# Long convolution by FFT and a gated MLP in one kernel: the first half of a batch's transform moved beside the second half of the one before it, and the last inverse step in two matmul passes instead of three for 17 of 48 tiles

## The chip, the core and the metric

One core of a Trainium2 chip runs the whole program. Its engines are named as in the profile: PE (TensorE, matmuls), PEld (its weight loads), DVE (VectorE), ACT (ScalarE), POOL (GpSimd) and SP (SyncE, which here only issues DMAs). The metric is device time in microseconds (us) of one execution, the median of the runs shown.

## The reference

```python
X = np.fft.rfft(x, axis=1)                       # x: 8 batches, 3008 positions, 256 channels
Y = X * (filt_r + 1j * filt_i)[None]
h = np.fft.irfft(Y, n=3008, axis=1).reshape(24064, 256) @ w_in     # 256 x 2048
out = (h * (1.0 / (1.0 + np.exp(-1.702 * h)))) @ w_out             # 2048 x 256
```

All is float32. A sequence of 3008 is transformed as 64 x 47, with dense matrices.

## The kernel before

The work of a batch `b` is a transform (`fft`, four steps of matmuls with pointwise work between), then six tiles `t` of up to 512 tokens, for which `signal` or `turned_signal` makes the last inverse step, and `mlp` the two products of the MLP. A tile has 16 chunks `fc`; a chunk has 6 matmuls into `h` (L784) and 6 into `o` (L808), two ACT gelus (L787, L788) and one DVE subtraction (L789). Every matmul runs in float32r; to keep float32's precision, operands are split into a high and a low part, and a product is the sum of high x high, high x low and low x high. `mm3` does that in three matmuls. A packed form does it in two: where the contraction fills only 64 partitions, high and low parts of the data are stacked in 128 partitions, and one matmul makes two halves of 64 rows that ACT and DVE then add.

**The transform.** `packed` (batches 2 to 7, counted from 0) is its first half: `fetch` loads a piece of `x` (512 KB, six per batch), `butterfly` makes sums and differences of it on POOL (L519), `split` divides them into high and low parts (ACT L525, POOL L526), `transform` multiplies (L537) and sends the result to DRAM (`a_d`). The second half has 16 steps `i`: `forward(i)` multiplies (`s2`, L588), ACT and DVE merge the two halves (`merge`, L596, L597), DVE multiplies with the filter, POOL adds (L612), DVE and POOL split the product again into `zy` (L616, L617); `backward(i)` multiplies `zy` (`i2`, L588), merges and stores to DRAM (`b_d`). The data of a batch goes through `a_d` and `b_d`, so its steps follow each other; the first half of batch `b + 1` began when the second half of batch `b` had ended.

**The last inverse step.** `turned_signal` loads `br` from `b_d`, splits it (ACT L739, POOL L740), multiplies it with `mm3` (L305 to L307, `i1`), transposes on DVE (L748, `zt`), turns the tile through DRAM (`z_d`, one store and four loads into `y`), and splits it (`split_off`: ACT L719, POOL L720).

**What sets the order.** The program is written as generators: at each chunk a table says how many steps of the transform (`COSTS`) and of the coming tiles (`due`, offsets `at` in chunks) are recorded. A scheduler then places each instruction in its engine's queue; each engine runs its queue strictly in that order, and waits at its head. Tiles in SBUF come from rings: `raw` (seven buffers of 4 KB a partition, among them the pieces of `x`) and `half` (seven of 2 KB). PE, too, runs in the recorded order.

Of the kernel before, what the change touches and what calls it, by code (L numbers as in the profile page):

```python
# [24 lines left out]
COSTS = [[0.746] * 12 + [1.212] * 2 + LATER] + [[0.8] * 4 + [0.675] * 24 + [1.3] * 2 + LATER] * 7  # L25
# [5 lines left out]
def _tables():  # L31
# [72 lines left out]
    tabs = [t1_0, d_0, e_0, np.eye(P), sign, t1, t1_s, t2, de]  # L104
# [4 lines left out]
WIDTHS = {"t1_0": P, "d_0": 2 * Q, "e_0": 192, "eye": P, "sign": NS, "t1": P, "t1_s": P, "t2": P, "de": 4 * Q}  # L109
# [58 lines left out]
def tile_kernel(  # L168
# [291 lines left out]
    def fft(b):  # L460
# [106 lines left out]
        yield from packed() if b > 1 else thrice()  # L567
# [68 lines left out]
        keep(4)  # L636
        if b == 1:
            nc.gpsimd.memset(zy[0].bitcast(F32), 0.0)
        for i in range(2):
            load(i)  # L640
            load_f(i)

        for i in range(2):
            yield
        for i in range(17):
            if i < 16:
                yield from forward(i)
            if i:
                yield from backward(i - 1)
        b_of[b] = b_d  # L650
# [63 lines left out]
    def split_off(y, m, q, to=None):  # L714

        to = y[:, :, m, q] if to is None else to
        src = y[:, 1, m, q].bitcast(F32)
        with tc.issue_after(gelu[-1]):
            nc.scalar.copy(to[:, 0], src)  # L719
        nc.gpsimd.tensor_tensor(to[:, 1], src, to[:, 0].bitcast(F32), ALU.subtract)  # L720

    def turned_signal(b, t, y):
# [20 lines left out]
        zt = sb.tile([P, 8, 4, 32], F32, tag="raw", name=f"zt_{b}_{t}", bufs=7)  # L743
        for m in range(2):
            ps = ring("f", [P, 2, D], f"i1_{b}_{t}_{m}")
            mm3(ps, t2h, t2l, *es[m])
            to = zt[:, :, 2 * m : 2 * m + 2].rearrange("p c q i -> p q c i")
            nc.vector.transpose(to, ps.rearrange("p q (c i) -> p q c i", c=8))  # L748
            yield
        z_d = dram.tile([P, 8, P], F32, tag="z_d", name=f"z_d_{b}_{t}")  # L750
        load_in(z_d, zt.rearrange("p c q i -> p c (q i)"))
        yield
        src = z_d.rearrange("(a j) (k g) e -> g j k a e", a=4, g=4)
        for g in range(4):
            dst = y[32 * g : 32 * g + 32, 1].bitcast(F32)
            load_in(dst.rearrange("p k (a e) -> p k a e", a=4), src[g])
        yield
        for m in range(2):
            if t < 5 or b % 2:
                split_off(y, m, slice(0, 512))  # L760
# [4 lines left out]
            elif t == 5:  # L765
                split_off(y, m, slice(0, 352))
                split_off(y, m, slice(384, 416), y[:, :, m, 352:384])
                split_off(y, m, slice(416, 480), carry[:, :, m])
            yield

    def mlp(b, t, y, nb, sums):
# [7 lines left out]
        def first(fc):  # L779
# [3 lines left out]
            for n, (kc, wk, yk) in enumerate([(k, *q) for k in range(2) for q in ((0, 0), (0, 1), (1, 0))]):  # L783
                nc.tensor.matmul(ps[:, :w], wi_sb[half][:, wk, kc, c], y[:, yk, kc, :w], start=n == 0, stop=n == 5)  # L784
# [53 lines left out]
    ys, t2_two, gelu = {}, [], []  # L838
# [117 lines left out]
```

## Time and profile before

| what | before |
|---|---|
| time, median of 3 runs (lowest to highest) | 2334.91 us (2334.2 to 2335.23) |
| time of the profiled execution | 2334.13 us |
| span of its instructions | 2332.3 us |
| PE busy | 2324.5 us (100%) |
| DVE, ACT, POOL busy | 1607.8, 1439.8, 1128.0 us |
| DMA, mean over the span | 125 GB/s |

The span runs from the first to the last profiled instruction; the time of the execution holds 1.8 us more. "Busy" is the time in which an engine had at least one instruction at work. A matmul's own duration in the profile is longer than the distance to the next one, since matmuls are pipelined, so for PE the distance between starts is what counts.

### The profile page before, as it was taken

The page shows a single profiled execution, that of the slowest core. Times are in us where ns is not written, and L with a number is a line of the kernel's source. Part 1 is how long each engine was busy: PE and PEld are TensorE (multiplying, and loading weights), DVE is VectorE, ACT ScalarE, POOL GpSimd, SP SyncE. Part 2 cuts the span into 40 slices and gives each one's busy share as a digit, 9 for nine tenths or more (in the row PEclk, how much of TensorE's full clock was granted, in tenths as well). Part 3 has the DMA queues.
Part 4 walks back from the last instruction along what each step waited for, and adds up shares of the span by engine and source line. Part 5 has one row for each costly group of instructions (what it writes and reads, how often), then busy time and mean ns, then how long its engine had stood idle before and what let it go on. Part 6 is the DMA issues. An engine that isn't in the chain of part 4 may idle for free.

```text
span 2332.3 us, 32211 instructions
## 1 busy us (share of the span) xinstructions
PE 2324.5 (100%) x10630; PEld 1944.9 (83%) x10630; DVE 1607.8 (69%) x2404; ACT 1439.8 (62%) x2654; POOL 1128.0 (48%) x999
## 2 busy tenths in 40 slices
PE   9999999999999999999999999999999999999999
PEld 7878898888888889888888888988888888888887
DVE  7978866688667885678855887568876688623222
ACT  6666657666675666756676666766657666544443
POOL 3035546466564665556654565736657466311010
PEclk9999999999999999999999999999999999999999
DMA  9265545566455664556545554555655465411100
GB/s 338 82 192 111 111 107 146 134 135 135 109 145 125 144 140 127 154 121 139 127 133 141 133 128 117 153 134 125 138 134 145 118 138 118 101 52 52 57 28 19
DMA packets 189238, 290.75 MB, mean 125 GB/s; under 512 B 18576, under 2 KB 125200, under 8 KB 189072
## 3 DMA queue, kind: packets, MB, share of 16 engines
q1 hardware_dynamic: 112368, 178.20, 26.5%
q0 software_dynamic: 46592, 44.05, 11.4%
q10 hardware_dynamic: 30112, 66.44, 11.1%
q8 instruction: 85, 1.39, 0.3%
q14 instruction: 81, 0.66, 0.1%
HBM read 173.80 MB, written 114.82 MB: 124 GB/s over the span
## 4 chain that ended last, share of the span: by engine, by line
PE 93%; DVE 0%; ACT 0%; issue 0%
PE o L808 42%; PE h L784 42%; PE s L588 2%; PE i L588 2%; PE s L537 1%; PE i L305 1%; PE i L307 1%; PE i L306 1%; PE i L700 0%; PE bt L671 0%; PE s L585 0%; PE s L586 0%; PE i L586 0%; PE i L585 0%; DVE out L816 0%; ACT gh L787 0%
## 5 line engine op out<-in xcount | busy, mean ns | idle before, releaser
L784 PE MATMUL h<-y,wi 128*128 128x512 f32 (+1 forms) x4608 | 1177.3, 385 | 0.1
L784 PEld LDWEIGHTS h<-y,wi 128*128 128x128 f32 x4608 | 858.9, 188 | 165.2 <-DVE gl L789 1.0
L789 DVE TENSOR_TENSOR gl<-h,gh 128x512 fp32r<-128x512 f32 (+1 forms) x768 | 520.7, 678 | 495.4 <-ACT h L788 467.9
L808 PE MATMUL o<-gh,wo 128*128 128x512 f32 (+1 forms) x3072 | 839.2, 385 | 1.2 <-ACT gh L787 1.2
L787 ACT ACTIVATE gh<-h 128x512 fp32r<-128x512 f32 (+1 forms) x768 | 452.2, 589 | 606.6 <-PE h L784 462.9
L808 PEld LDWEIGHTS o<-gh,wo 128*128 128x128 f32 x3072 | 573.4, 188 | 111.6 <-ACT gh L787 1.9
L808 PE MATMUL o<-gl,wo 128*128 128x512 f32 (+1 forms) x1536 | 481.6, 385 | 0.5 <-DVE gl L789 0.5
L788 ACT ACTIVATE h<-h 128x512 f32<-128x512 f32 (+1 forms) x768 | 449.0, 585 | 0.0
L617 POOL TENSOR_TENSOR zy<-c_buf,zy 48x512 fp32r<-48x512 f32 x224 | 316.0, 1411 | 75.0 <-DVE zy L616 63.3
L808 PEld LDWEIGHTS o<-gl,wo 128*128 128x128 f32 x1536 | 287.5, 188 | 56.5 <-DVE gl L789 1.1
L612 POOL TENSOR_TENSOR c_buf<-c_buf,u_buf 112x512 f32<-112x512 f32 x112 | 144.6, 1291 | 229.2 <-DVE c_buf L611 229.2
L574 POOL DMA_DIRECT2D zy<-a_d x224 | 130.3, 586 | 232.5 <-PE s L588 92.9
L740 POOL TENSOR_TENSOR bl<-br,bh 128x512 fp32r<-128x512 f32 x80 | 107.1, 1353 | 246.5 <-ACT bh L739 204.7
L720 POOL TENSOR_TENSOR y<-y 128x512 fp32r<-128x512 f32 (+1 forms) x86 | 105.3, 1230 | 205.2 <-ACT y L719 193.8
L597 DVE TENSOR_TENSOR c_buf<-s,c_buf 48x512 f32<-48x512 f32 x224 | 154.1, 688 | 33.3 <-ACT c_buf L596 28.6
L596 ACT COPY c_buf<-s 48x512 f32<-48x512 f32 x224 | 130.2, 581 | 70.9 <-PE s L588 58.5
L596 ACT COPY b<-i 48x512 f32<-48x512 f32 x224 | 130.1, 581 | 58.4 <-PE i L588 46.5
L597 DVE TENSOR_TENSOR b<-i,b 48x512 f32<-48x512 f32 x224 | 153.8, 687 | 15.1 <-ACT b L596 10.3
L540 DVE TENSOR_TENSOR a<-s,a 64x512 f32<-64x512 f32 x144 | 99.0, 688 | 63.3 <-ACT a L539 60.5
L616 DVE CAST zy<-c_buf 48x512 fp32r<-48x512 f32 x224 | 109.4, 488 | 39.8 <-POOL c_buf L612 34.6
L605 DVE TENSOR_TENSOR u_buf<-c_buf,f_buf 48x512 f32<-48x512 f32 x112 | 110.3, 985 | 3.8
L539 ACT CAST a<-s 64x512 fp32r<-64x512 f32 x144 | 83.7, 581 | 40.8 <-PE s L537 26.6
(126 smaller groups left out, 1789.5 us busy)
## 6 DMA issues: line engine op xcount, KB each, us to landing
f_buf<-fs SPq DMA_DIRECT2D x224, 192.0 KB, 3.4
zy<-a_d POOLq DMA_DIRECT2D x224, 192.0 KB, 3.7
a_d<-a ACTq DMA_DIRECT2D x144, 256.0 KB, 3.0
x<-in_x_dram SPq DMA_DIRECT2D x47, 512.0 KB, 5.5
out_dram<-out SPq DMA_DIRECT2D x43, 512.0 KB, 3.7
b_d<-b ACTq DMA_DIRECT2D x112, 192.0 KB, 2.8
br<-b_d SPq DMA_DIRECT2D x84, 256.0 KB, 4.5
z_d<-zt SPq DMA_DIRECT2D x40, 512.0 KB, 2.7
```

What stands on the lines that cost most here:

```text
L574: nc.gpsimd.dma_start(zy[0][64 * k : 64 * k + 48, i % 2].rearrange("p k s d -> p (k s) d"), src)
L596: nc.scalar.copy(dst[h], ps[o])
L597: nc.vector.tensor_tensor(dst[h], ps[h], dst[h], ALU.add)
L605: nc.vector.tensor_tensor(u2[64:Q], u1[0:48], f_i[0:48], ALU.mult)
L612: nc.gpsimd.tensor_tensor(u1, u1, u2, ALU.add)
L616: nc.vector.tensor_copy(y[h, k], u1[h])
L617: nc.gpsimd.tensor_tensor(y[o, k], u1[h], y[h, k].bitcast(F32), ALU.subtract)
L784: nc.tensor.matmul(ps[:, :w], wi_sb[half][:, wk, kc, c], y[:, yk, kc, :w], start=n == 0, stop=n == 5)
L787: nc.scalar.activation(gh[:, :w], ps[:, :w], AF.Gelu_apprx_sigmoid)
L788: gelu.append(nc.scalar.activation(ps[:, :w], ps[:, :w], AF.Gelu_apprx_sigmoid).ins)
L789: nc.vector.tensor_tensor(gl[:, :w], ps[:, :w], gh[:, :w].bitcast(F32), ALU.subtract)
L808: ins = nc.tensor.matmul(pos[m][:, :w], wb[:, P * m : P * m + P], g[:, :w], start=first_one, stop=last_one)
```

## The change

Three things are edited together.

First, `fft` now gives two generators, the first half and the second (`two`). A list of moments (`steps`, from `SPACED` and `FIRST_LEG`) replaces `COSTS`. From batch 3 on the first half of batch `b` begins while the second half of batch `b - 1` still runs: 4 of its 24 matmul steps lie beside it for batch 3 and 6 for batches 4 to 7, within the last 16 and 24 chunks of it.

Second, the first half gets its own memory, `s1_pool`: two slots for pieces of `x`, three for results, one for the even sums. Before, all these took buffers of the rings `raw` and `half`. `fetch` now runs at odd `n`, when the last split of a slot is recorded.

Third, for the tiles that `is_packed` names (t = 3, 4, 5 of b = 3 to 6, and t = 1 to 5 of b = 7: 17 tiles) `packed_passes` replaces `turned_passes`: four matmuls of 512 columns instead of six, with four merges, and sums and differences on POOL (into `yf`) after the turn through DRAM.

```diff
-COSTS = [[0.746] * 12 + [1.212] * 2 + LATER] + [[0.8] * 4 + [0.675] * 24 + [1.3] * 2 + LATER] * 7
+SPACED = [(0, 0, 32), (16, 4, 20), (24, 6, 17)]
+FIRST_LEG = [0.746] * 12 + [1.212] * 2 + LATER
...
+                s1_pool.append(const.tile([P, 6, 4, D], F32, tag="b_t", name="s1_pool"))
...
-                    xs[c] = raw(f"x_{b}_{c}").rearrange("p (j i) d -> p j i d", j=2)
+                    xs[c] = s1_pool[0][:, c % 2].rearrange("p (j i) d -> p j i d", j=2)
...
-                        if n % 2 == 0:
+                        if n % 2:
                             fetch(n // 2 + 2)
...
+    def is_packed(b, t):
+        return b > 2 and t > 2 or b == B - 1 and t > 0
...
+    def packed_passes(b, t, zt):
...
+        br = [raw(f"br{j}_{b}_{t}") for j in range(2)]
+        for j in range(2):
+            n = NH * j + 4 * t
+            for k in range(2):
+                load_in(br[j][halves(k)], b_of[b][n : n + 4].rearrange("n k d -> k n d"))
+        yield
+        es = {}
+        for m in range(2):
+            for j in range(2):
+                e, src = half(f"z{j}_{b}_{t}_{m}"), br[j][:, 2 * m : 2 * m + 2]
+                with tc.issue_after(gelu[-1]):
+                    nc.scalar.copy(e, src)
+                nc.gpsimd.tensor_tensor(e[64:P], src[64:P], e[64:P].bitcast(F32), ALU.subtract)
+                es[m, j] = e
+            yield
+        zt.append(sb.tile([P, 8, 4, 32], F32, tag="raw", name=f"zt_{b}_{t}", bufs=7))
+        for m in range(2):
+            uv = sb.tile([P, 2, D], F32, tag="half", name=f"uv_{b}_{t}_{m}", bufs=7)
+            for j in range(2):
+                ps, h, o = ring("f", [P, 2, D], f"i1_{b}_{t}_{m}_{j}"), halves(j), halves(1 - j)
+                with tc.issue_after(begin[-1]):
+                    nc.tensor.matmul(ps, t2_w[0][:, j].rearrange("p a c -> p (a c)"), es.pop((m, j)), start=True, stop=True)
+                nc.scalar.copy(uv[h], ps[o])
+                nc.vector.tensor_tensor(uv[h], ps[h], uv[h], ALU.add)
...
+            for j in range(2):
+                ins = nc.gpsimd.tensor_tensor(yj[:, :, j], uv[:, :, 0], uv[:, :, 1], ALU.subtract if j else ALU.add)
...
+            if is_packed(b, t):
+                at = (-8, -4, -3, -2, -1, 0, 1, 2, 4, 8, 9, 10)
```

What moves stands below at one place, the end of tile t = 4 of batch 3, where the second half of the transform of batch 4 ends and the first half of that of batch 5 now runs beside it. In the names, `s2_4_15_1` is batch 4, step 15, half 1; `zy` holds batch 4 here, with `c_buf1`, `c_buf2` and `c_buf0` for steps 13, 14 and 15; `e1_5_5` is the split for batch 5, n = 5, half 1; `y_3_5` is the tile that the MLP takes next. In the changed kernel's lines L523 is `butterfly`, L530 `split`, L632 the sum in `forward`, L637 the split into `zy`, L815 the new sums and differences, L730 `split_off`, L825 the copies of left-over tokens into `y`.

POOL's queue before, from the split of step 13 to that of step 15:

```order
L617 TENSOR_TENSOR zy_1451<-c_buf1_83,zy_1451 48x512 x2
L612 TENSOR_TENSOR c_buf2_84<-c_buf2_84,u_buf0_85 112x512
L617 TENSOR_TENSOR zy_1451<-c_buf2_84,zy_1451 48x512 x2
L720 TENSOR_TENSOR y_3_5_10601<-y_3_5_10601 128x512
L764 CAST y_3_5_10601<-carry_88 128x2x32 x2
L720 TENSOR_TENSOR y_3_5_10601<-y_3_5_10601 128x512
L764 CAST y_3_5_10601<-carry_88 128x2x32 x2
L612 TENSOR_TENSOR c_buf0_82<-c_buf0_82,u_buf1_86 112x512
L519 TENSOR_TENSOR ev_5_0_11240<-x_5_0_11177 128x512
L617 TENSOR_TENSOR zy_1451<-c_buf0_82,zy_1451 48x512 x2
```

and now, from the split of step 14 to that of step 15 and the copies:

```order
L632 TENSOR_TENSOR c_buf2_84<-c_buf2_84,u_buf0_85 112x512
L637 TENSOR_TENSOR zy_1452<-c_buf2_84,zy_1452 48x512 x2
L530 TENSOR_TENSOR e1_5_5_11297<-s1_pool_3223,e1_5_5_11297 64x512
L523 TENSOR_TENSOR s1_pool_3223<-s1_pool_3223 128x512
L815 TENSOR_TENSOR yf_3_5_11075<-uvt_3_5_10962 128x2x256 x2
L632 TENSOR_TENSOR c_buf0_82<-c_buf0_82,u_buf1_86 112x512
L523 TENSOR_TENSOR s1_pool_3223<-s1_pool_3223 128x512
L530 TENSOR_TENSOR e0_5_6_11326<-s1_pool_3223,e0_5_6_11326 64x512
L730 TENSOR_TENSOR y_3_5_10582<-yf_3_5_11075,y_3_5_10582 128x512 x2
L637 TENSOR_TENSOR zy_1452<-c_buf0_82,zy_1452 48x512 x2
L825 CAST y_3_5_10582<-carry_88 128x2x32 x4
```

Between the two splits into `zy` there stood eight POOL instructions, four of them short copies; now there are nine, all long: the split `e1_5_5`, two sums of `x`, another split, the tile's own sums and splits.

SP's queue now, around the load of `x` that the first L523 above reads:

```order
L211 DMA z_d_3_5_10909<-zt_3_5_10785 128x1024
L211 DMA uvt_3_5_10962<-z_d_3_5_10909 32x8x128 x4
L211 DMA f_buf_81<-fs_80 48x1024 x2
L211 DMA s1_pool_3223<-in_x_dram 128x1024
L211 DMA f_buf_81<-fs_80 48x1024 x2
L888 DMA out_0_dram<-out_3_4_11258 256x1x512
```

This load writes the slot that `e1_5_5` reads, and so waits for it. Before, this load went to a free buffer of the ring `raw`.

PE's queue before, up to the second inverse matmul of step 15:

```order
L784 MATMUL h_3_5_1_11153<-y_3_5_10601,wi_0_583 128x512 x6
L588 MATMUL i2_4_15_0_11089<-zy_1451,de_sb_79 128x512
L808 MATMUL o_3_4_0_10775<-gl_3_4_14_11101,wo_1_984 128x512
L808 MATMUL o_3_4_0_10775<-gh_3_4_15_11124,wo_1_984 128x512 x2
L808 MATMUL o_3_4_1_10776<-gl_3_4_14_11101,wo_1_984 128x512
L808 MATMUL o_3_4_1_10776<-gh_3_4_15_11124,wo_1_984 128x512
L588 MATMUL i2_4_15_1_11111<-zy_1451,de_sb_79 128x512
```

and now:

```order
L870 MATMUL o_3_4_0_10831<-gl_3_4_15_11190,wo_1_984 128x512
L870 MATMUL o_3_4_1_10832<-gl_3_4_15_11190,wo_1_984 128x512
L608 MATMUL i2_4_15_0_11154<-zy_1452,de_sb_79 128x512
L608 MATMUL i2_4_15_1_11158<-zy_1452,de_sb_79 128x512
L541 MATMUL s1_5_3_0_11200<-e0_5_3_10996,t1_two_3224 128x512
L541 MATMUL s1_5_3_1_11227<-e1_5_3_11101,t1_two_3224 128x512
L845 MATMUL h_3_5_0_11209<-y_3_5_10582,wi_0_583 128x512 x3
L845 MATMUL h_3_5_1_11238<-y_3_5_10582,wi_0_583 128x512 x3
```

All of tile 4's matmuls now stand ahead of the two inverse matmuls, and all of tile 5's behind them. In PE's order now 104 matmuls of 512 columns stand from `s2_4_14_1` (the last forward matmul of step 14) up to `i2_4_15_1`; before there were 111. The same rows stand one more time, with batches 6, 7 and tile t = 5 of batch 5.

## Rows read from the trace of the kernel before

**Rows 1.** The page's head and PE's part of its first section.

```profile
span 2332.3 us, 32211 instructions
PE 2324.5 (100%) x10630; PEld 1944.9 (83%) x10630; DVE 1607.8 (69%) x2404; ACT 1439.8 (62%) x2654; POOL 1128.0 (48%) x999
```

**Rows 2.** All waits of PE: who waited for whom, us in total, times, longest.

```profile
PE o L808 <- ACT gh L787: 1.2, 2, 1.0
PE idle L326 <- DVE zero L373: 1.1, 1, 1.1
PE o L808 <- DVE gl L789: 0.5, 1, 0.5
PE i L426 <- POOL c_buf L458: 0.3, 1, 0.3
```

**Rows 3.** Chain that ended last: start us, us, what.

```profile
892.55 2.77 PE o L808 x16
...
1169.46 4.08 PE h L784 x18
...
2323.35 4.55 PE o L808 x20
```

**Rows 4.** Busy us of each engine (and instructions) in stretches; clock, DMA, GB/s.

```profile
core 0: us, PE busy (x) PEld busy (x) DVE busy (x) ACT busy (x) POOL busy (x), PEclk, DMA share, GB/s
...
60.00:170.00 110.00, 108.21 (x496) 88.30 (x495) 94.79 (x161) 71.51 (x136) 22.73 (x15) 1.00 0.45 136
...
920.00:1160.00 240.00, 240.00 (x1067) 199.28 (x1067) 189.17 (x275) 156.70 (x284) 139.19 (x126) 1.00 0.56 136
...
2057.00:2100.00 43.00, 43.00 (x195) 36.00 (x194) 12.73 (x19) 18.90 (x36) 5.26 (x5) 1.00 0.15 46
```

**Rows 5.** PE's groups by shape, the last inverse step: busy us, mean ns.

```profile
L307 PE MATMUL i<-bh,t_two 128*128 128x512 f32 x80 | 31.2, 390 | 0.0
L305 PE MATMUL i<-bh,t_two 128*128 128x512 f32 x80 | 31.1, 389 | 0.0
L306 PE MATMUL i<-bl,t_two 128*128 128x512 f32 x80 | 31.1, 389 | 0.0
```

**Rows 6.** POOL's groups by shape: busy us, mean ns, idle before.

```profile
L617 POOL TENSOR_TENSOR zy<-c_buf,zy 48x512 fp32r<-48x512 f32 x224 | 316.0, 1411 | 75.0 <-DVE zy L616 63.3 <-PE o L808 3.0
L612 POOL TENSOR_TENSOR c_buf<-c_buf,u_buf 112x512 f32<-112x512 f32 x112 | 144.6, 1291 | 229.2 <-DVE c_buf L611 229.2
...
L740 POOL TENSOR_TENSOR bl<-br,bh 128x512 fp32r<-128x512 f32 x80 | 107.1, 1353 | 246.5 <-ACT bh L739 204.7 <-DMA a_d<-a 22.2 <-issue 9.8
L720 POOL TENSOR_TENSOR y<-y 128x512 fp32r<-128x512 f32 x74 | 98.0, 1326 | 200.0 <-ACT y L719 191.8 <-issue 6.8
...
L526 POOL TENSOR_TENSOR e<-x,e 64x512 fp32r<-64x512 f32 x72 | 92.7, 1288 | 14.9 <-ACT e L525 8.9 <-PE s L537 0.7 <-PE h L784 0.7
L519 POOL TENSOR_TENSOR x<-x 128x512 f32<-128x512 f32 x36 | 46.5, 1293 | 2.7
```

**Rows 7.** ACT's and DVE's groups by shape: busy us, mean ns, idle before.

```profile
L596 ACT COPY b<-i 48x512 f32<-48x512 f32 x224 | 130.1, 581 | 58.4 <-PE i L588 46.5 <-PE i L586 3.7 <-PE o L808 2.8
...
L739 ACT CAST bh<-br 128x512 fp32r<-128x512 f32 x80 | 48.1, 613 | 8.1 <-DMA br<-b_d 7.9
...
L597 DVE TENSOR_TENSOR b<-i,b 48x512 f32<-48x512 f32 x224 | 153.8, 687 | 15.1 <-ACT b L596 10.3
```

**Rows 8.** Timeline of PE and POOL, step 15 of batch 4: start us, us.

```profile
1154.79 0.39 PE L588 MATMUL s<-zy,de_sb 128*128 128x512 f32 x1
...
1160.30 1.29 POOL L519 TENSOR_TENSOR ev<-x 128x512 f32<-128x512 f32 x1
1162.04 2.80 POOL L617 TENSOR_TENSOR zy<-c_buf,zy 48x512 fp32r<-48x512 f32 x2 [0.45 <-DVE zy L616]
1164.92 1.29 POOL L519 TENSOR_TENSOR x<-x 128x512 f32<-128x512 f32 x1
...
1167.03 0.39 PE L588 MATMUL i<-zy,de_sb 128*128 128x512 f32 x1
```

**Rows 9.** Timeline of PE and POOL, an earlier step of batch 4.

```profile
1043.27 0.39 PE L588 MATMUL s<-zy,de_sb 128*128 128x512 f32 x1
...
1048.54 2.89 POOL L617 TENSOR_TENSOR zy<-c_buf,zy 48x512 fp32r<-48x512 f32 x2 [0.53 <-DVE zy L616]
```

**Rows 10.** Loads of `x` on SP: who waited for them, and time to landing.

```profile
L208 SPq DMA_DIRECT2D x<-in_x_dram x49: 327/423/1421, 0.7 to 1801.8; - x49
...
who waited for it (us, times):
  POOL ev L519: 5.2, 3
  ACT xh L480: 4.7, 3
...
DMA to landing us min/median/max: 3.4/5.4/7.8
```

**Rows 11.** Timeline of PE at the start: start us, us, idle before.

```profile
1.06 3.78 PE L326 MATMUL idle<-zero 128*128 128x512 f32 x8 [1.06 <-DVE zero L373]
4.64 3.61 PE L386 MATMUL s<-tab,x 128*128 128x128 f32 x20
```

More of the change, by code (lines that the diff above doesn't have):

```diff
@@ L517, in butterfly @@
                     c, j = divmod(n, 2)
-                    sums[n] = xs[c][:, 1] if j else sb.tile([P, 2, D], F32, tag="half", name=f"ev_{b}_{c}", bufs=7)
+                    sums[n] = xs[c][:, 1] if j else s1_pool[0][:, 5, 2 * (c % 2) : 2 * (c % 2) + 2]
                     nc.gpsimd.tensor_tensor(sums[n], xs[c][:, 0], xs[c][:, 1], ALU.subtract if j else ALU.add)
@@ L565, in packed, with two @@
                     yield
-        yield from packed() if b > 1 else thrice()
+        def two():
+            keep(len(late))
+            if b == 1:
+                nc.gpsimd.memset(zy[0].bitcast(F32), 0.0)
+            for i in range(2):
+                load(i)
+                load_f(i)
+            for i in range(2):
+                yield
+            for i in range(17):
+                if i < 16:
+                    yield from forward(i)
+                if i:
+                    yield from backward(i - 1)
+            b_of[b] = b_d
         b_d = dram.tile([48, 64, D], F32, tag="b_d", name=f"b_d{b}")
@@ L634, in backward, with halves @@
                 yield
[L636 to L650, printed above, removed]
+        return packed() if b > 1 else thrice(), two()
+    def halves(k):
+        return slice(64 * k, 64 * k + 64)
+    def is_packed(b, t):
+        return b > 2 and t > 2 or b == B - 1 and t > 0
     def signal(b, t, y):
@@ L837, in tile_kernel @@
     b_t = []
-    ys, t2_two, gelu = {}, [], []
+    ys, t2_two, gelu, s1_pool, t2_w, begin = {}, [], [], [], [], []
     def start(b, t):
@@ L882, in tile_kernel @@
             due.setdefault(n, []).append(j)
-    legs, passed, since = [], 0, 0
-    for b in range(B - 1):
-        upto = sum(NFC * width(i) for i in range(6 * b + 6)) - 4 * LEAD - ((18 if b > 1 else 12) * width(6 * b + 5) if b else 26)
-        legs.append((COSTS[b], list(COSTS[b]), upto))
-    nxt = [fft(1)]
+    steps, passed, since = [], 0, 0
+    for b in range(1, B):
+        upto = sum(NFC * width(i) for i in range(6 * b)) - 4 * LEAD - ((18 if b > 2 else 12) * width(6 * b - 1) if b > 1 else 26)
+        if b == 1:
+            at = np.cumsum(FIRST_LEG) * (upto / sum(FIRST_LEG))
+            one, two = at[:12], at[12:]
+        else:
+            early, beside, alone = SPACED[min(b, 4) - 2]
+            first = since - 4 * early
+            last = since + 4 * alone
+            if not early:
+                since = first = first + 4 * 5.5
+            lead = first - 4 * np.array([5.0, 4.0, 2.2, 1.1])
+            one = [*lead, *(first + (since - first) * np.arange(beside) / max(beside, 1))]
+            one += list(since + (last - since) * (np.arange(24 - beside) / (23 - beside)))
+            two = [last + 4 * 1.5, last + 4 * 3, *(last + 4 * 4 + (upto - last - 4 * 4) * np.cumsum([0.0, *LATER[1:]]) / sum(LATER[1:]))]
+        one = [*one, two[0]]
+        steps += [(when, b, which) for which, ats in enumerate((one, two)) for when in ats]
+        since = upto
+    steps.sort()
+    legs = {}
     for n, (i, fc) in enumerate(turns):
```

78 lines of the change are left out of this document (49 added, 29 removed).

## Prediction

> **What bounds the kernel now.** I read the page's head first: PE is busy in 2324.5 of 2332.3 us, each other engine in 69% of the span or less [rows 1]. A busy PE is not yet a bound, so the second view is the list of all its waits: four rows, 3.1 us together [rows 2]. The third is the chain that ended last. It runs over PE's matmuls, and its pieces give the price of one: 18 matmuls of 512 columns take 4.08 us, 16 take 2.77 where some are narrower [rows 3], so a full one takes 0.2267 us. The windows place the remaining idleness: 1.8 us of PE's lie between 60 and 170, and from 920 to 1160 PE is busy in 240.00 of 240 us, beside DVE at 79%, ACT at 65% and POOL at 58% [rows 4]. So the time is the sum of PE's matmuls. It falls by what is taken from that sum, and grows by every wait that PE does not have today.
>
> **What is taken away.** Each of the 17 packed tiles has four matmuls where six stood: today there are 80 of each of three kinds, two of each kind for each of 40 tiles [rows 5]. That is 34 matmuls of 512 columns, at 0.2267 us [rows 3] 7.7 us. This is the whole gain: the overlap of the transforms removes no matmul, and PE waits for nothing that it could bring forward. 7.7 us are 0.33%; I take 0.2%, 4.7 us, as what a measurement of this kernel tells from no change.
>
> **What is added beside PE.** A packed tile costs ACT two more casts (0.61) and four copies (0.58), 3.5 us, and DVE four additions (0.69), 2.8 us [rows 7]. On POOL, four splits of 64 partitions (1.29, as the row of L526) and two sums (1.29, as L519) replace two splits (1.35): 5.0 us more [rows 6]. A tile lasts 16 x 12 x 0.2267 = 43.5 us, so in the stretch from 920 to 1160 ACT comes to 73%, DVE to 85%, POOL to 70%: under the tile's time, the MLP's matmuls cover it, and I cost the load at nothing. If an engine filled up, its excess over 43.5 us a tile would be PE's wait. In the last batch POOL is busy in 5.26 of 43 us [rows 4], and its five tiles are free. Two more loads and one `yf` a tile are hidden in the same way, and so is a start-up table that grows by a sixth.
>
> **Where the order does not cover it.** An average of 70% hides a place where one chain runs through POOL alone. I looked for the places where PE's next operand has the longest chain behind it, and found one that the change makes much worse: step 15 of batch 4 (and of batch 6). From the start of `s2_4_14_1` up to `i2_4_15_1` PE has 104 matmuls to do, 23.6 us. In that time the following must pass, one after the other, since POOL keeps its order:
>
> - From the forward matmul to the end of the second split into `zy`. The trace has this chain: from 1154.79 to 1162.04 + 2.80 = 1164.84, 10.05 us, one sum of `x` among it [rows 8]; without such neighbours from 1043.27 to 1048.54 + 2.89, 8.16 us [rows 9]. In the changed order POOL has splits and sums of `x` ahead of it, so I take 10.05.
> - The split `e1_5_5`, 1.29 us [rows 6].
> - The load of `x` into the slot that this split has just freed. Before, a load of `x` had a free buffer and was early: POOL waited for it three times, 5.2 us in all. It lands after 5.4 us (3.4 to 7.8) [rows 10]. Now it can't be issued before the split has ended, and POOL's next instruction needs it. 5.4 us in which POOL stands, with the tile's sums, whose data are there, queued behind.
> - Then POOL, without a pause: two sums of `x` (1.29 each), two of the tile (1.29 each, the nearest form), the addition of step 15 (1.29), one split (1.29), two splits of the tile (1.33 each), the two splits into `zy` (2.8 to 2.9): 13.2 us [rows 6, 8].
>
> Sum 10.05 + 1.29 + 5.4 + 13.2 = 29.9; with 0.08 between one POOL instruction and the next (1164.84 to 1164.92 [rows 8]), eight times, 30.5. PE has 23.6. It would wait **6.9 us**, and behind `i2_4_15_1` stand all matmuls of tile 5, so nothing fills the gap. Before, PE came to the first of the two inverse matmuls at 1167.03, 2.2 us after POOL had finished at 1164.84 [rows 8]: the same place was the narrow one, but with room. From both sides: with 8.16, a load of 3.4 and no gaps the chain is 26.0 and the wait 2.4 us; with a load of 7.8 and 1 us more queueing it is 10.3 us. I take 6.9, since the trace's own last step has the 10.05 and the load's median is nearer to most of its loads than its ends. Batch 6 has the same 104 matmuls and the same POOL rows, so it counts twice: 13.8 us. For the other batches the same sum comes out covered: in batch 3 POOL has no split of `x` in that stretch, so no load is held back; batch 7 has no batch behind it; and batch 5 has 125 matmuls, some of them narrower, 27.9 us, and other POOL work that covers part of its load, so that its chain takes some 26.
>
> The tables of `steps` and `at` move other things too; the matmuls of the packed tiles stand at least 33 matmuls, 7.5 us, behind the gelu that releases their cast, and a cast and two POOL splits take 3.2 us, so I cost them at nothing.
>
> **Sum.** The profiled execution took 2334.13 us, 0.8 below the median. 2334.1 - 7.7 + 13.8 = 2340.2; carried to the median, **2341.0 us**: slower by 0.26%.
>
> **Rivals.**
> 1. The waits don't come, or are hidden (the loads land early, POOL is ahead of where I put it): what is left is the matmuls. 2334.9 - 7.7 = 2327.2 us. For it: PE waits nowhere today [rows 2], and 17 tiles less two passes is sure. Against it: the chain must be 6.9 us shorter at both places, which is more than the load. This is the other side; it decides where the two waits together stay under 3 us.
> 2. Short waits, 2.4 to 5 us each: the chain's start is the 8.16 of [rows 9] and the loads land in 4 to 5 us. 2334.9 - 7.7 + 4.8 to 10 = 2332 to 2337, no change that can be told.
> 3. The wait costs more than its length. The longest wait of PE behind the start-up is 1.0 us [rows 2], and the granted clock is 1.00 in the stretches shown [rows 4]; what a wait of 5 us does, no row shows. At the start, after idleness, eight matmuls of 512 columns take 3.58 us from the first to the next kind (1.06 to 4.64), 0.45 each instead of 0.227 [rows 11]. If PE came out of each wait like that, 8 to 18 matmuls (18 is the block of tile 5's that follows) at 0.22 more would add 1.8 to 4.0 us twice: 2344.6 to 2349 us.
>
> The Trainium skill ("TensorE: Matmul & The Clock Gate", The HAM clock gate) says that the clock is the slow one by default and falls back to it after idleness, from 2.4 to 1.2 GHz. By that rule rival 3 is what happens; the 1.0 us waits of this trace are too short to test it.
>
> **How the numbers follow.** Waits of 5 to 9 us each, no more: 50% (2337.2 to 2345.2). Rival 1: 13%; rival 2: 22%; rival 3, or still longer queues: 15%. The range leaves out rival 1 and the upper half of rival 3: 2331 to 2347.5 us. Within the likeliest case alone it is 2337 to 2345. Faster by over 0.2% is under 2330.2: rival 1 less its edge, 12%. Within 0.2%, up to 2339.6: rival 2 and a quarter of the likeliest case, 35%. Slower: 53%.
>
> **What would show it.** In the profile after: PE's list of waits should hold two rows or so with waits of 4 to 7 us each, on POOL, for `zy` (L637) or `y`, near 1160 to 1175 and near 1725 to 1740 us; POOL should wait there for the DMA `s1_pool<-in_x_dram`, some 5 us twice or more, at L523; PE's matmuls of `i1` should be 68 of the new kind and 46 of each of three old ones. If PE's list stays at some 3 us, rival 1 was right and the chain's first link or the load was over-costed. If the granted clock falls below 1.00 behind a wait, rival 3 was. I would be wrong about the whole place if POOL took the tile's sums before the load, or if PE found matmuls to do in the gap; and wrong upwards if some other operand came late as well, above all the merges that free PSUM for `s1_5_3_1`, behind the two inverse matmuls.

## The result

The changed kernel takes **2366.45 us** (median of 4 runs, 2365.98 to 2368.97) against 2335.02 (2334.2 to 2335.23): ratio 1.0138, 95% interval 1.0126 to 1.0151. It is slower by 31.4 us where I forecast 6, and outside my range. One execution of `fetch_early` below, 3329.08 us at a granted clock of 0.65, is left out of its median.

The page's head and PE's part of it, after, as in [rows 1]:

```profile
span 2364.5 us, 32237 instructions
PE 2332.9 (99%) x10596; PEld 1937.7 (82%) x10596; DVE 1692.4 (72%) x2474; ACT 1499.4 (63%) x2758; POOL 1227.8 (52%) x1067
```

34 matmuls are gone (10630 to 10596), and DVE has 84.6 us more to do where 17 x 2.8 = 48 were forecast. The rest of the change shows first in PE's waits, as in [rows 2] (us in total, times, longest):

```profile
PE h L845 <- DVE gl L851: 7.3, 10, 1.2
PE i L608 <- POOL zy L637: 5.6, 4, 2.2
PE i L761 <- DVE s_pool L545: 3.5, 3, 1.2
PE o L870 <- DVE gl L851: 3.4, 3, 1.6
PE o L870 <- ACT gh L849: 2.1, 4, 1.0
PE s L608 <- DVE b L617: 1.7, 4, 0.5
...
PE s L541 <- DVE b L617: 0.6, 2, 0.4
```

Four rows stood there before, 3.1 us; now there are 11 rows, 26.6 us. The row that I forecast is the second. Two of the 11, 1.4 us together, stood there before; the others, all short and most of them on DVE, I had not forecast. The windows, as in [rows 4], say where (the first row is from the kernel before, the others from the changed one):

```profile
core 0: us, PE busy (x) PEld busy (x) DVE busy (x) ACT busy (x) POOL busy (x), PEclk, DMA share, GB/s
1050.00:1160.00 110.00, 110.00 (x487) 91.06 (x486) 95.92 (x139) 70.96 (x128) 68.25 (x65) 1.00 0.58 137
...
1050.00:1160.00 110.00, 105.18 (x453) 83.87 (x452) 93.44 (x125) 76.02 (x136) 78.72 (x66) 1.00 0.59 135
1160.00:1190.00 30.00, 25.66 (x102) 19.87 (x101) 21.89 (x30) 15.73 (x29) 20.13 (x19) 0.89 0.44 114
...
1740.00:1780.00 40.00, 35.84 (x146) 28.34 (x145) 30.68 (x41) 23.78 (x44) 24.33 (x22) 0.91 0.46 134
...
1180.60:1187.40 6.80, 4.80 (x10) 3.27 (x11) 2.79 (x5) 2.94 (x5) 4.21 (x8) 0.50 0.44 130
...
1800.00:2100.00 300.00, 300.00 (x1372) 254.10 (x1371) 203.92 (x300) 185.11 (x347) 148.91 (x132) 1.00 0.48 111
```

PE now idles 4.82 us between 1050 and 1160, although over this stretch DVE is busy in 93.44 of 110 us, 85%, ACT in 69% and POOL in 72%. Before, DVE was busy in 95.92 us there, 87%, and PE waited nowhere. Behind 1800, with the packed tiles of batches 6 and 7, PE does not wait at all.

The list of waits is not the whole loss. Taking from the trace how much later than 0.227 us after the one before each matmul of PE starts, the new delays are 39.1 us: **14.4** at the two places of the prediction (1175 to 1190 and 1762 to 1776), **20.6** in short waits between 1050 and 1740, and **4.1** between 280 and 612, where no tile is packed. 39.1 - 7.7 = 31.4 us, the whole change. The table under the experiments splits every run in this way.

### The profile page after: what moved, and what is told of

Read it like the earlier page. It is cut to its first block, busy times and chain, and to the rows that moved or that the text cites. A ratio compares the mean times of both kernels' runs of the same rounds, so it can differ in the third digit from the quotient of the medians.

```text
span 2364.5 us, 32237 instructions
## 1 busy us (share of the span) xinstructions
PE 2332.9 (99%) x10596; PEld 1937.7 (82%) x10596; DVE 1692.4 (72%) x2474; ACT 1499.4 (63%) x2758; POOL 1227.8 (52%) x1067
## 3 DMA queue, kind: packets, MB, share of 16 engines
q0 software_dynamic: 46592, 44.05, 11.6%
## 5 line engine op out<-in xcount | busy, mean ns | idle before, releaser
L637 POOL TENSOR_TENSOR zy<-c_buf,zy 48x512 fp32r<-48x512 f32 x224 | 312.9, 1397 | 77.6 <-DVE zy L636 67.8
L632 POOL TENSOR_TENSOR c_buf<-c_buf,u_buf 112x512 f32<-112x512 f32 x112 | 144.9, 1294 | 179.0 <-DVE c_buf L631 176.1
L530 POOL TENSOR_TENSOR e<-s_pool,e 64x512 fp32r<-64x512 f32 x144 | 191.2, 1328 | 47.7 <-ACT e L529 34.3
L617 DVE TENSOR_TENSOR c_buf<-s,c_buf 48x512 f32<-48x512 f32 x224 | 154.1, 688 | 51.4 <-ACT c_buf L616 48.2
L617 DVE TENSOR_TENSOR b<-i,b 48x512 f32<-48x512 f32 x224 | 153.8, 687 | 27.8 <-ACT b L616 23.1
L636 DVE CAST zy<-c_buf 48x512 fp32r<-48x512 f32 x224 | 130.0, 581 | 37.2 <-POOL c_buf L632 31.6
L787 POOL TENSOR_TENSOR bl<-br,bh 128x512 fp32r<-128x512 f32 x46 | 60.7, 1332 | 137.1 <-ACT bh L786 130.8
L544 DVE TENSOR_TENSOR s_pool<-s,s_pool 64x512 f32<-64x512 f32 x144 | 99.0, 687 | 38.7 <-ACT s_pool L543 35.9
L523 POOL TENSOR_TENSOR s_pool<-s_pool 128x512 f32<-128x512 f32 x72 | 94.4, 1312 | 58.7 <-DMA s_pool<-in_x_dram 52.9
L625 DVE TENSOR_TENSOR u_buf<-c_buf,f_buf 48x512 f32<-48x512 f32 x112 | 110.0, 982 | 3.8
```

The source lines that it names most:

```text
L530: nc.gpsimd.tensor_tensor(es[n, h][o], src[t], es[n, h][t].bitcast(F32), ALU.subtract)
L617: nc.vector.tensor_tensor(dst[h], ps[h], dst[h], ALU.add)
L632: nc.gpsimd.tensor_tensor(u1, u1, u2, ALU.add)
L636: nc.vector.tensor_copy(y[h, k], u1[h])
L637: nc.gpsimd.tensor_tensor(y[o, k], u1[h], y[h, k].bitcast(F32), ALU.subtract)
```

## The experiments

Theory A: the packed tiles' work crowds the engines beside PE. Theory B: the new order of the transforms does it. "Places" are the two of the prediction, "short" the waits elsewhere between 900 and 2100, "early" those from 280 to 900, all in us, worked out as above.

| run | median us | ratio to before (95%) | places | short | early |
|---|---|---|---|---|---|
| after | 2366.45 | 1.0138 (1.0126 to 1.0151) | 14.4 | 20.6 | 4.1 |
| no_pack | 2339.56 | 1.0022 (1.0012 to 1.0031) | 0 | 0 | 4.2 |
| old_order | 2360.96 | 1.0122 (1.0102 to 1.0142) | 18.9 | 11.6 | 3.3 |
| old_order_last | 2334.98 | 1.0002 (0.9993 to 1.0010) | 0 | 0 | 3.4 |
| fetch_early | 2366.2 | 1.0137 (1.0117 to 1.0156) | 14.9 | 19.8 | 4.2 |
| x_in_ring | 2359.17 | 1.0104 (1.0089 to 1.0119) | 5.6 | 18.5 | 7.2 |
| no_yf | 2342.77 | 1.0036 (1.0023 to 1.0049) | 0 | 11.3 | 4.1 |
| no_zsub | 2362.04 | 1.0118 (1.0101 to 1.0135) | 16.5 | 13.6 | 4.2 |
| no_merge | 2340.86 | 1.0027 (1.0017 to 1.0038) | 2.5 | 6.5 | 3.9 |
| no_sum | 2344.32 | 1.0041 (1.0028 to 1.0055) | 6.0 | 7.0 | 4.1 |
| no_copy | 2349.34 | 1.0062 (1.0049 to 1.0076) | 13.2 | 5.2 | 4.0 |
| yf_on_dve | 2356.92 | 1.0090 (1.0076 to 1.0104) | 10.7 | 15.1 | 3.9 |
| plus_yf | 2339.90 | 1.0022 (1.0013 to 1.0031) | 0 | 0 | 4.3 |
| plus_merge | 2341.06 | 1.0024 (1.0015 to 1.0033) | 0 | 1.6 | 4.2 |
| plus_both | 2348.61 | 1.0055 (1.0042 to 1.0069) | 7.4 | 0 | 4.0 |
| plus_all | 2353.98 | 1.0083 (1.0068 to 1.0098) | 10.6 | 3.6 | 4.1 |
| packed_three | 2363.44 | 1.0122 (1.0105 to 1.0139) | 10.1 | 14.3 | 4.0 |
| before_last | 2332.40 | 0.9992 (0.9983 to 1.0001) | 0 | 0 | 0 |
| before_last_six | 2332.09 | 0.9988 (0.9979 to 0.9996) | 0 | 0.6 | 0.3 |

**Packing or order.** `no_pack` undoes the packing:

```diff
-        return b > 2 and t > 2 or b == B - 1 and t > 0
+        return False
```

> All tiles keep the three passes; the overlapped order of the transforms and their own buffer stay. The matmuls of the 17 tiles come back: +7.7 us. Theory A (the short waits of 0.2 to 1.6 us, 24.6 us together, come from the packed tiles' load on VectorE, ScalarE and GpSimd): all of them between 1060 and 1740 us go (about 20.8 us), the two waits on GpSimd near 1180 and 1768 us stay (14.4 us), so 2366.5 + 7.7 - 20.8 = 2353 us. Theory B (they come from the new order of the transforms alone): nothing goes, 2366.5 + 7.7 = 2374 us. Theory C (only both together crowd the engines): near A's time, but then the old order with packing shows none either.

`old_order` gives the transforms the spacing from before, with the packing kept:

```diff
+        elif True:
+            at = since + np.cumsum(OTHER_LEG) * ((upto - since) / sum(OTHER_LEG))
+            one, two = at[:28], at[28:]
         else:
```

> The steps of the transforms stand where they stood before the change (one transform after another, spaced by the old costs); the 17 packed tiles and the transforms' own buffer stay. Theory A (packing crowds the engines by itself): the two waits on GpSimd go, the short waits of 1060 to 1740 us stay, so 2335.0 - 7.7 + 20.8 = 2348 us. Theory B (the order is the cause of all waits) and theory C (only both together): no waits, 2335.0 - 7.7 = 2327 us, faster than before by 0.33%.

The new order together with its two slots for `x` costs 4.6 us, nearly all of it in early waits (4.2); packing in the old order, which has the slots too, costs 26 us (33.7 us of waits). So theories B and C are out. A is right that packing makes the waits, but its times, 2353 and 2348 us, both miss: without packing the two places have no wait either, though I had expected their 14.4 us to stay. And under the old order, packing makes PE wait near the same places, here for `y` itself (PE's waits in `old_order`):

```profile
PE h L846 <- POOL y L826: 12.9, 2, 7.7
PE h L846 <- DVE gl L852: 3.6, 5, 1.1
```

**The load of `x`.** `fetch_early` asks for it a step sooner; `x_in_ring` does so too and gives it a buffer of the shared ring.

```diff
-                        if n % 2:
+                        if n % 2 == 0:
                             fetch(n // 2 + 2)
```

```diff
-                    xs[c] = s1_pool[0][:, c % 2].rearrange("p (j i) d -> p j i d", j=2)
+                    xs[c] = raw(f"x_{b}_{c}").rearrange("p (j i) d -> p j i d", j=2)
```

> The changed kernel with one edit: the next piece of x is asked for one step of the transform sooner (two matmul groups of the pair), so that its load is not in the chain that GpSimd waits for. Theory of the prediction (load of x, 5.4 us, in the chain of the two places): the waits near 1180 and 1768 us, 7.3 and 7.1 us with the fall of the clock behind them, shrink by the 5.4 us of load and lose the low clock, so about 12 us go: 2354 us; the short waits elsewhere stay. Rival (GpSimd's own work is what is late, the load only the wait that ends last): less than 4 us goes, 2363 to 2366 us.

> The changed kernel with the pieces of x of batches 2 to 7 in the shared ring of seven buffers, asked for one step sooner, in place of two fixed slots, so that a load need not wait for GpSimd's last subtraction on the slot. If the load of x in GpSimd's queue is what makes the two places late: 3.8 us less there each and no low clock, 2366.5 - 10 = 2356 us, and GpSimd's wait for x (52.9 us in all) shrinks. Rival (as with the earlier call: nothing moves, as GpSimd's own work or VectorE is late): 2364 to 2368 us. If the ring is too short for it, longer than 2368 us.

The earlier call changes nothing: in the timeline of `fetch_early` the load is still issued only when the split that reads the slot has ended (1165.39 + 1.29), and POOL still stands for it.

```profile
1165.39 1.29 POOL L530 TENSOR_TENSOR e<-s_pool,e 64x512 fp32r<-64x512 f32 x1
...
1166.70 0.35 SPq L211 DMA_DIRECT2D s_pool<-in_x_dram  x1
...
1170.27 1.29 POOL L523 TENSOR_TENSOR s_pool<-s_pool 128x512 f32<-128x512 f32 x1 [3.59 <-DMA s_pool<-in_x_dram]
```

With a buffer of its own the load left before that split, and POOL's last split into `zy` ended ahead of the inverse matmul:

```profile
1163.45 0.37 SPq L211 DMA_DIRECT2D x<-in_x_dram  x1
...
1178.13 2.84 POOL L637 TENSOR_TENSOR zy<-c_buf,zy 48x512 fp32r<-48x512 f32 x2 [0.42 <-DVE zy L636]
...
1181.42 0.61 PE L608 MATMUL i<-zy,de_sb 128*128 128x512 f32 x2
```

So the slot, not the place in the queue, held the load back, and it is 8.8 of the 14.4 us of the two places. The waits from 280 to 340 go as well (the two slots made them), but the fuller ring costs 7.2 us from 600 to 900.

**Which part of packing.** Four parts are left out of the changed kernel, one at a time. `no_yf` (the split reads what the load brought):

```diff
-                ins = nc.gpsimd.tensor_tensor(yj[:, :, j], uv[:, :, 0], uv[:, :, 1], ALU.subtract if j else ALU.add)
```

`no_zsub`:

```diff
-                nc.gpsimd.tensor_tensor(e[64:P], src[64:P], e[64:P].bitcast(F32), ALU.subtract)
```

`no_merge`, where the transpose reads `ps`; `no_sum` takes out the second of the two lines, and `no_copy` puts VectorE's copy in their place:

```diff
-                nc.scalar.copy(uv[h], ps[o])
-                nc.vector.tensor_tensor(uv[h], ps[h], uv[h], ALU.add)
```

```diff
+                nc.vector.tensor_copy(uv[h], ps[h])
```

`yf_on_dve` leaves nothing out; it has `nc.vector` for `nc.gpsimd` in the line of `no_yf`.

> The changed kernel without the sums and differences of two halves that make a packed tile's y (two GpSimd instructions, 2.5 us, per packed tile; the output is then not the reference's). Theory S (GpSimd's own queue is what is late at the two places near 1180 and 1768 us): 2.5 us less there each and no low clock, about 2366.5 - 9 = 2357 us. Theory D (GpSimd's instructions beside VectorE's make VectorE's longer, from 0.69 to 1.2 to 1.8 us, and the matmuls wait for the late gl): a third of the packed tiles' added GpSimd work is gone, so about a third of the 20 us of short waits more: near 2350 us. Theory L (VectorE's and ScalarE's own added instructions crowd their queues): only the two places gain, 2357 us or more.

> The changed kernel without the subtractions that make the lower half of a packed operand (four GpSimd instructions of 1.3 us per packed tile; ScalarE's copy fills both halves, so the second pass multiplies by the wrong part and the output is not the reference's). Theory D: with 5.2 us of GpSimd less per packed tile VectorE's instructions keep their length and most of the short waits go: 2366.5 - 20 = 2346 us or less. Theory L: the short waits stay but for a few, 2360 us or more (the two places may still gain, as GpSimd has less to do).

> The changed kernel without the merge of the two halves of a packed product (four copies on ScalarE, 0.58 us, and four sums on VectorE, 0.69 us, per packed tile; the transpose reads PSUM directly, so half of the product is left out and the output is not the reference's). Theory L: the short waits go with the 2.8 us of VectorE and 2.3 us of ScalarE per packed tile: 2366.5 - 20 = 2346 us. Theory D: the lengthened instructions remain, under 10 us go: 2357 us or more. If both this and the run without the subtractions gain 15 us or more, the engines are crowded together and either relief suffices.

> The changed kernel with the packed tile's sums and differences on VectorE in place of GpSimd (2.5 us less on GpSimd, 1.4 us or more on VectorE per packed tile). Theory S (GpSimd's queue is late at the two places): the 14.4 us of waits there go as they went without those sums, and the short waits elsewhere grow a little: 2350 to 2356 us. Theory L (VectorE is the engine that is late everywhere): what GpSimd gains VectorE loses: 2362 us or more.

> The changed kernel without VectorE's four sums per packed tile (0.69 us each, half of the product left out, the output is not the reference's); ScalarE's copies stay. Without both, 25.6 us went. If VectorE's queue is what delays gl: nearly all of it, 2341 to 2346 us. If ScalarE's copies are as much to blame: about half, 2353 us.

> The changed kernel without ScalarE's four copies per packed tile (0.58 us each); VectorE copies its own half from PSUM in place of the sum (the other half of the product is left out, the output is not the reference's). If VectorE's queue is what delays gl: little goes, 2358 us or more. If ScalarE's copies are as much to blame: about half, 2353 us. If ScalarE alone: 2341 to 2346 us.

Against 2366.5 us: the sums of `yf` give back 23.7 us, the merges 25.6 (VectorE's half of them alone 22.1, ScalarE's alone 17.1), but the four subtractions, twice the work of `yf` on POOL, only 4.4. Theory D alone does not explain the cost, then (the last section comes back to it). S gave too little for `yf`, and L says nothing of it: either relief takes most of the waits away, though 11.3 and 6.5 us of short ones stay. Moved to VectorE, the sums still cost 14 us, between the forecasts of S and L.

One caution: the scheduler places the queues of every run anew, so leaving out a part changes the order too. In `no_yf`, at the first place, POOL has the tile's two splits and its short copies ahead of the sum of `x` that stood for its load, and does not stand there.

**One cause or a meeting.** Starting from `no_pack`, parts are added to three passes in the same 17 tiles: `plus_yf` the two POOL instructions and their buffers (first edit), `plus_merge` the copies and VectorE's instructions (second), `plus_both` both, `plus_all` two more casts and splits besides (third).

```diff
+                ins = nc.gpsimd.tensor_tensor(yj[:, :, j], uv[:, :, j], uv[:, :, j], ALU.add)
```

```diff
+                for h in (halves(0), halves(1)):
+                    nc.scalar.copy(uv[h], ps[h])
+                    nc.vector.tensor_tensor(uv[h], ps[h], uv[h], ALU.max)
```

```diff
+                    nc.scalar.copy(e2, src)
+                nc.gpsimd.tensor_tensor(e2[64:P], src[64:P], e2[64:P].bitcast(F32), ALU.subtract)
```

> The overlapped order with three passes everywhere (2339.6 us), and beside it, in the 17 tiles, a packed tile's two GpSimd instructions between the load and the split of y (each half added to itself, so y is doubled and the output is not the reference's) with their two buffers. Theory X (no part does it alone: the waits come when the sums on GpSimd and the merges on ScalarE and VectorE meet in queues that run in order): no more than the 9 us that packing without the merges cost, 2341 to 2349 us. Theory Y (the sums on GpSimd alone make the waits, as leaving them out took 24 us away): 2339.6 + 20 = 2360 us.

> The same base (2339.6 us) with a packed tile's four copies on ScalarE and four two-operand instructions on VectorE ahead of the transpose in the 17 tiles (the larger of a number and its copy, so nothing changes in the output). Theory X: alone they cost no more than the 11 us that packing without the sums cost, 2341 to 2350 us. Theory Z (the merges alone make the waits, as leaving them out took 26 us away): 2339.6 + 20 = 2360 us.

> The same base with both additions (y is doubled, so the output is not the reference's). Theory X: far more than the two costs added, as the changed kernel has them: 2339.6 + 23 to 27 us = 2363 to 2367 us. If the costs only add up (no meeting in the queues): the sum of the two runs above. If it is below 2350 us, something else of the packed tiles makes the waits (four subtractions, their loads, the earlier start).

> Three passes with the sums on GpSimd and the merges (2348.6 us), and in each of the 17 tiles two copies more on ScalarE and two subtractions more on GpSimd, as many as a packed tile has to make its operands (y is doubled as there; the two extra operands are not read). Theory X (each addition costs more the fuller the queues are): 2358 us or more, towards the 2374 us of the changed kernel with its matmuls put back. If 2352 us or less, what is left (some 20 us) belongs to the packed tiles' earlier start, to their two more loads, or to TensorE's shorter work.

0.3 us, 1.5 us, both 9.0 us, all 14.4 us. Neither is a cause by itself, and together they cost five times their sum: theory X in kind, though at 2348.6 us, not the 2363 of its forecast. What comes back is 7.4 us of waits at the two places; of the 20.6 us of short waits none comes back, and 3.6 with `plus_all`. For the short ones, then, the meeting is argued from what leaving parts out gave, and not shown by putting them in. At the first place `gl` is late first and POOL's splits behind it (timeline of PE in `plus_both`):

```profile
1171.60 0.74 PE L876 MATMUL o<-gl,wo 128*128 128x512 f32 x2 [1.40 <-DVE gl L857]
1174.60 0.49 PE L608 MATMUL i<-zy,de_sb 128*128 128x512 f32 x1 [0.86 <-POOL zy L637]
1175.94 0.50 PE L608 MATMUL i<-zy,de_sb 128*128 128x512 f32 x1 [0.84 <-POOL zy L637]
```

**What the saved matmuls were worth.** `packed_three` issues one of each two matmuls of a packed tile twice:

```diff
+                for _ in range(j + 1):
                     with tc.issue_after(begin[-1]):
                         nc.tensor.matmul(ps, t2_w[0][:, j].rearrange("p a c -> p (a c)"), e, start=True, stop=True)
```

> The changed kernel with one of the two matmuls of each half tile issued twice (the second writes the same product over the first), so that TensorE does as many matmuls as with three passes (34 more, 7.7 us) and everything else of the packed tiles stays. If the waits are set by the other engines' queues, TensorE's extra work is done in what were its waits: 2366.5 us, at most 2369 us; then the saved matmuls were worth nothing in the crowded tiles. If the waits stand beside the matmuls: 2366.5 + 7.7 = 2374 us.

2363.4 us, 3.0 us *less* than with 34 matmuls fewer, though that is under the 0.2% that I took as the bound. The saved 7.7 us had only become waits: those at the two places are 4.3 us shorter here (10.1 for 14.4), the short ones 6.3 (14.3 for 20.6).

**How far packing can go.** `old_order_last` is `old_order` with the last batch alone packed; `before_last` has the old buffers too; `before_last_six` packs tiles three to five of batch 6 besides.

```diff
-        return b > 2 and t > 2 or b == B - 1 and t > 0
+        return b == B - 2 and t > 2 or b == B - 1 and t > 0
```

> The old order of the transforms, with packing in tiles one to five of the last batch alone, where no transform runs beside it: 10 matmuls fewer, -2.3 us. The changed trace shows no wait behind 2100 us in the packed tiles, so all theories say 2335.0 - 2.3 = 2332.7 us, unless the transforms' own two-slot buffer for x costs something in the old order too (rival: 2335 or above).

> The kernel before (its order and its buffers for the transforms) with packing in tiles one to five of the last batch alone: 10 matmuls fewer, -2.3 us. The old order with the two-slot buffer and the same five packed tiles waited 3.1 us between 280 and 340 us, where the kernel before does not wait; if the slots are the cause, that goes here: 2334.8 - 2.3 = 2332.5 us. If the wait has another cause (the packed tiles' longer program, code that sits elsewhere): 2335 us.

> The kernel before with packing in the last batch (2332.4 us) and in tiles three to five of batch six: 6 matmuls fewer again, -1.4 us. The old order with all 17 tiles packed waited 1.0 us between 1800 and 2100 us, where these three stand: 2332.4 - 1.4 + 1.0 = 2332.0 us; without that wait 2331.0 us; if the shared ring of seven buffers gets too short for transforms and packed tiles together, more than 2333 us.

In the first of them the early waits, 3.4 us with the two slots, take away the 2.3 us that it could have gained. `before_last` gains 2.1 us, as its 10 matmuls say, with an interval that just takes in 1; `before_last_six`, with 16 matmuls less (3.6 us), gains 2.7, faster than both kernels by its interval, though by 0.12%, less than the 0.2% that I took as the bound:

```profile
span 2330.7 us, 32300 instructions
PE 2321.5 (100%) x10614; PEld 1940.3 (83%) x10614; DVE 1639.4 (70%) x2438; ACT 1466.5 (63%) x2704; POOL 1174.1 (50%) x1031
```

## Why the prediction was wrong

**The step that failed** is the one in "What is added beside PE": "under the tile's time, the MLP's matmuls cover it, and I cost the load at nothing", with its test that only an engine that filled up would make PE wait. Measured, packing costs 26.9 us (2366.45 - 2339.56), 34.6 with the saved matmuls, while DVE is at 85% from 1050 to 1160, as I had put it, and was at 87% there before, without a wait. A share over a whole tile does not bound a wait; what meets in the queues within a few microseconds does. Near 1060 us, in batch 3, the timeline of the changed kernel shows how:

```profile
1057.87 2.53 POOL L815 TENSOR_TENSOR yf<-uvt 128x512 f32<-128x512 f32 x2 [5.62 <-DMA uvt<-z_d]
1060.37 1.28 POOL L632 TENSOR_TENSOR c_buf<-c_buf,u_buf 112x512 f32<-112x512 f32 x1
...
1061.69 0.87 DVE L636 CAST zy<-c_buf 48x512 fp32r<-48x512 f32 x2 [3.16 <-POOL c_buf L632]
1062.59 1.66 DVE L625 TENSOR_TENSOR u_buf<-c_buf,f_buf 48x512 f32<-48x512 f32 x1
1064.28 0.69 DVE L851 TENSOR_TENSOR gl<-h,gh 128x512 fp32r<-128x512 f32 x1
...
1065.03 1.66 PE L845 MATMUL h<-y,wi 128*128 128x512 f32 x6 [0.19 <-DVE gl L851]
```

POOL stands for the packed tile's load, does its two sums, and only then the transform's sum L632. DVE has the cast of that sum at the head of its queue, idles 3.16 us, and has `gl` behind it; then it does everything late, and PE, a chunk or two ahead of `gl`, waits. So a packed instruction on one engine is idle time on the next. Here PE waits only 0.19 us; near 1650 the same chain (DVE idle for 3.96 us) makes 0.77. Near 1080 and 1670 DVE does not idle and is late all the same, as the last section shows; what share of the 20.6 us each kind has was not taken apart. Added to three passes, the sums or the merges alone find room (`plus_yf`, `plus_merge`: under 2 us), both together do not (`plus_both`). The Trainium skill ("TensorE: Matmul & The Clock Gate", the table of its head) lists ScalarE's, VectorE's and GpSimd's queues as strictly first in, first out; the rows near 1060 agree.

**Right: matmuls.** 68 of the new kind and 46 of each of the three old ones, as said (PE's groups, as in [rows 5]):

```profile
L761 PE MATMUL i<-z,t_w 128*128 128x512 f32 x68 | 26.7, 393 | 3.5 <-DVE s_pool L545 3.5
L308 PE MATMUL i<-bh,t_two 128*128 128x512 f32 x46 | 18.0, 392 | 0.5 <-ACT bh L786 0.5
```

But the 7.7 us are a gain only where PE does not wait: `before_last` has nearly all of its 2.3, and `packed_three` shows that here they were worth nothing. And these matmuls, whose wait I costed at nothing too, waited 3.5 us themselves: not for the operands that I had looked at, but for DVE's merge L545, which reads a PSUM tile of the same ring.

**Right: the place; its sum by luck.** The two places cost 7.3 and 7.1 us, where I said 6.9 each (the first row is `s2_4_14_1`):

```profile
1154.47 0.39 PE L608 MATMUL s<-zy,de_sb 128*128 128x512 f32 x1
...
1165.21 1.29 POOL L530 TENSOR_TENSOR e<-s_pool,e 64x512 fp32r<-64x512 f32 x1
1170.32 1.29 POOL L523 TENSOR_TENSOR s_pool<-s_pool 128x512 f32<-128x512 f32 x1 [3.81 <-DMA s_pool<-in_x_dram]
...
1179.09 0.73 PE L870 MATMUL o<-gl,wo 128*128 128x512 f32 x2 [1.57 <-DVE gl L851]
...
1180.75 2.59 POOL L637 TENSOR_TENSOR zy<-c_buf,zy 48x512 fp32r<-48x512 f32 x2
...
1182.06 0.80 PE L608 MATMUL i<-zy,de_sb 128*128 128x512 f32 x1 [2.23 <-POOL zy L637]
1183.40 0.80 PE L608 MATMUL i<-zy,de_sb 128*128 128x512 f32 x1 [0.54 <-POOL zy L637]
```

POOL's run from the load to the last split is 13.0 us (1170.32 to 1183.34), against 13.2. The load holds POOL for 3.8 us, not 5.4. The whole chain, from 1154.47 on, is 28.9 us, not 30.5, and so 5.3 beyond PE's 23.6; that the low clock behind it brought the place to 7.3 is luck. PE's waits are 4.3 us, of which DVE's 1.57 was not in the chain; most of the other 3 us is **rival 3**: from 1180.6 to 1187.4 the granted clock is 0.50 (1.2 GHz of 2.4); it fell within the second of the two longer waits, two matmuls behind the first, and ten matmuls take 4.80 us there, not 2.27. I gave that 15%; it happened at both places (0.91 over 1740 to 1780). The Trainium skill ("TensorE: Matmul & The Clock Gate", The HAM clock gate) says that the clock falls back after idleness; the row at 1180.60 agrees. Nor do the order and the load make the place wait by themselves: without packing, or without `yf` alone, PE does not wait there, though in `no_pack` POOL still stands for a load of `x`:

```profile
1156.75 3.75 POOL L523 TENSOR_TENSOR s_pool<-s_pool 128x512 f32<-128x512 f32 x2 [4.00 <-DMA s_pool<-in_x_dram]
```

The tile's sums were in my list of POOL's chain; that PE does not wait without them I had not worked out (by my sum the chain would still be 4.2 us too long). The ends of the transforms of batches 3 and 7 stayed covered, as said; rivals 1 and 2 fell with the waits.

**Not seen at all:** the two slots for `x` cost 3 to 4 us from 280 us on, in every kernel that has them, and none in `before_last` or, at 280 to 340, in `x_in_ring`; in `no_pack` POOL stands there for the load:

```profile
284.72 3.91 POOL L523 TENSOR_TENSOR s_pool<-s_pool 128x512 f32<-128x512 f32 x3 [3.61 <-DMA s_pool<-in_x_dram]
```

I had looked for late loads at the end of each transform and not at its start. My last sentence, wrong upwards "if some other operand came late as well", was the right fear, at 20.6 us. Merges of the kind that I named (L545, L617) are 5.8 us of the waits, but not at `s1_5_3_1`; most of the rest is `gl`.

**Open.** How the parts of packing make the short waits is in part argued. From `no_pack` to `packed_three`, which have the same matmuls, are 23.9 us; the sums and merges make 9.0 of them, the operands' casts and splits 5.4. The other 9.5 us belong to what was not tried apart, such as the earlier start, two more loads, and the order in which four halves are made.

## What to carry to other kernels

Beside a saturated engine, shares of busy time do not say what more the others can take: at 85%, 69% and 72% PE waited, where it had not at 87%, 65% and 62% before. Each queue runs in order here, and a transform that crosses three of them hands a delay on. Ask of an added instruction what stands behind it on its engine while it waits for its own operand, and count two additions together, not one by one. Then put the cheaper form only where no such chain runs beside it (here the last tiles), and see that a buffer is free before its load is wanted, since asking earlier for a full one moves nothing.

## What the hardware showed that I had not expected

VectorE's two-operand instructions on SBUF are longer beside POOL's. In the changed kernel's timeline, three of them with POOL's splits beside them, and what PE waits for behind them:

```profile
1075.99 1.17 DVE L625 TENSOR_TENSOR u_buf<-c_buf,f_buf 48x512 f32<-48x512 f32 x1
1077.19 1.67 DVE L630 SCALAR_TENSOR_TENSOR u_buf<-c_buf,f_buf 48x512 f32<-48x512 f32 x1
1078.90 0.69 DVE L851 TENSOR_TENSOR gl<-h,gh 128x512 fp32r<-128x512 f32 x1
1079.50 1.79 DVE L631 TENSOR_TENSOR c_buf<-c_buf,f_buf 112x512 f32<-112x512 f32 x1
...
1081.82 0.67 DVE L851 TENSOR_TENSOR gl<-h,gh 128x512 fp32r<-128x512 f32 x1
...
1076.69 1.62 POOL L752 TENSOR_TENSOR z<-br,z 64x512 fp32r<-64x512 f32 x1
1079.44 1.30 POOL L752 TENSOR_TENSOR z<-br,z 64x512 fp32r<-64x512 f32 x1
...
1082.55 1.66 PE L845 MATMUL h<-y,wi 128*128 128x512 f32 x6 [1.25 <-DVE gl L851]
```

`gl`, which reads PSUM, keeps its 0.69 us; L631 takes 1.79 and L630 1.67 us. Of the 112 instructions of L631, the 79 with none of POOL's two-operand work beside them take 0.69 us on average, the 25 that have it beside them for most of their time 1.35 us. The Trainium skill ("GPSIMD Engine Reference", Specifications) names this contention, for VectorE's instructions with two SBUF inputs; the rows agree. L630 and L631 are 19.6 of the 37 us that DVE is beyond my forecast. The casts L636, with one operand in SBUF, are longer too (0.42 us on average alone, 0.68 beside POOL's work), another 20.6 us.

Here this length is what PE waits for. From 1074.55 DVE works without a pause up to the second `gl`; L625, L630 and L631 take 2.6 us more than 0.69 each, and PE waits 1.25 us. In `no_zsub`, which has none of these splits, L630 and L631 take 0.69 and 0.68 us there:

```profile
1076.26 0.69 DVE L630 SCALAR_TENSOR_TENSOR u_buf<-c_buf,f_buf 48x512 f32<-48x512 f32 x1
...
1078.19 0.68 DVE L631 TENSOR_TENSOR c_buf<-c_buf,f_buf 112x512 f32<-112x512 f32 x1
```

PE waits neither there nor near 1670, which is 4.1 us of the short waits. Yet over the whole kernel `no_zsub`, with 93 us less work on POOL, gained only 4.4 us, since other waits came up in its queues (2.6 us near 1121, 4.4 near 1708).
